# A block scheme with seven products for the MLP's first matmul, and decoding dealt to two passes

## The chip, the cores and the metric

The kernel runs on one core of one Trainium2 chip. The metric is device time in microseconds of one execution; the profile is of one execution. TensorE (PE) multiplies, with its weight loads (PEld) beside it; VectorE (DVE), ScalarE (ACT) and GpSimd (POOL) work on elements; SyncE (SP) issues most DMAs.

## What is computed

Clustered attention over 2 batches, 8 heads, 768 positions of 64, and then two MLP layers over all 1536 tokens (512 wide, 2048 hidden), one behind the other:

```python
x = np.ascontiguousarray(attn_out.transpose(0, 2, 1, 3)).reshape(B * S, H * D)
# layer 1
h = x @ w_in
g = h * (1.0 / (1.0 + np.exp(-1.702 * h)))
x = g @ w_out
# layer 2
h = x @ w_in2
r = np.maximum(h, 0.0)
out = (r * r) @ w_out2
```

The four weight matrices come as 64-bit floats, so the kernel decodes them to 32 bits itself. Every matmul operand is split in two parts of the reduced format `fp32r`, `hi` (a rounded copy) and `lo` (what is left), and every product is three matmuls: hi*hi, hi*lo, lo*hi.

## The kernel before

Attention fills the first third of the span. It also decodes the first weights on the side and leaves x in `x1[b]`, one tile per batch of 768 tokens.

The MLP is four passes: layer 1 for batch 0, layer 1 for batch 1, layer 2 for batch 0, layer 2 for batch 1. A pass goes over 16 chunks of 128 hidden columns. For a chunk, `hidden` (L120) computes the first product into two PSUM banks, 12 matmuls of 512 columns and 12 of 256; `act.gate` (L677) applies the nonlinearity, ScalarE first and then a multiplication on VectorE; `act.split` (L686) makes `gh` on ScalarE and `gl` on VectorE; and `second` (L691) adds the chunk's share of the second product to six PSUM banks. `second` of a chunk is issued after `hidden` of the next one (`pend`), so that gate and split of a chunk have the time of a second product and a first product. At the end of a pass `finish` (L711) copies the six banks to `x1[b]` or stores them to the output. There are 8 banks: two for `hidden`, six for `second`.

A weight chunk is loaded by SP as 64-bit words (`w_dma`, L67, 512 KB, two buffers), ScalarE takes the absolute value (`magnitude`, L76), VectorE makes 32-bit floats of it in four steps (`decode`, L82: clamp, shift, sign, low bits), and `parts` (L100) splits it: ScalarE copies the high half, GpSimd subtracts for the low half. Each chunk of a layer needs this twice, for w_in and for w_out. A layer's decoded chunks stay in SBUF for both batches. The loop at L734 decodes layer 1 in the first pass and layer 2 in the second, one chunk per turn of the loop, in between gate and split in an order written out by hand. Each engine works strictly in the order of issue.

## Time and profile before

| what | value |
|---|---|
| time, median of 3 runs (lowest to highest) | 808.25 us (807.52 to 809.0) |
| the profiled execution: span from first to last instruction | 805.4 us |
| mean granted TensorE clock | 0.999 of full speed |
| mean DMA rate | 76 GB/s |

The page gives the profiled execution by its span; what lies before the first and after the last instruction is not in it. A share of busy time is a mean over stages: attention to about 263 us, then passes from about 270, 401, 536 and 670 us on. In a timeline, "x4" merges four instructions, and a row's duration runs to the end of the last; matmuls are pipelined, so the time that one costs is read from start to next start.

### The profile page before, as it was taken

Reading aid. Unit: us, or ns where it says so; the run is one execution under the profiler, and the core shown is the slowest. Engines: PE = TensorE matmul, PEld = TensorE weight load, DVE = VectorE, ACT = ScalarE, POOL = GpSimd, SP = SyncE. Lnnn points to the kernel's source line nnn. Section 1 sums busy time; section 2 is a strip of 40 time slices with the busy share of each in tenths; the row PEclk is TensorE's granted clock in tenths of the full one; section 3 lists DMA queues with packets and bytes.
Section 4 is the critical chain, followed back from the end, with each engine's and each line's share of the span. In section 5 each row is a group of like instructions: output and inputs, shape, how many; then the busy total and the mean of one; then the engine's idle time right before and its main releaser. Section 6 shows DMA issues by size and latency. Waiting matters only on the chain.

```text
span 805.4 us, 12494 instructions
## 1 busy us (share of the span) xinstructions
PE 794.0 (99%) x4647; PEld 694.2 (86%) x4647; DVE 571.1 (71%) x941; ACT 435.5 (54%) x927; POOL 203.6 (25%) x185
## 2 busy tenths in 40 slices
PE   8999999999999999999999999999999999999998
PEld 5899989989988888888888888888888888888886
DVE  7899999998898699999759999988222234222222
ACT  5898898888989545555534555554222233212222
POOL 1435535445436243323103232312000000000000
PEclk9999999999999999999999999999999999999999
DMA  8242542432311244343204434421000002000002
GB/s 231 87 131 56 161 123 63 136 105 53 82 27 34 74 131 130 117 130 121 79 27 131 128 110 131 130 81 51 1 1 1 0 1 79 1 1 0 1 1 78
DMA packets 40412, 60.89 MB, mean 76 GB/s; under 512 B 4224, under 2 KB 31648, under 8 KB 40352
## 3 DMA queue, kind: packets, MB, share of 16 engines
q1 hardware_dynamic: 35168, 52.98, 22.8%
q10 hardware_dynamic: 5184, 7.12, 2.6%
q8 instruction: 36, 0.59, 0.3%
q14 instruction: 24, 0.20, 0.1%
HBM read 46.18 MB, written 3.19 MB: 61 GB/s over the span
## 4 chain that ended last, share of the span: by engine, by line
PE 82%; DVE 9%; ACT 5%; DMA 2%; issue 1%; POOL 1%; ACTq 0%; DVEq 0%; POOLq 0%; SPq 0%
PE ph L129 31%; PE y L709 16%; PE y L700 10%; PE pa L442 5%; PE pt L417 5%; PE y L702 5%; DVE el L430 3%; PE ps L393 3%; PE ps L394 2%; DVE nm L399 2%; ACT e L408 2%; DMA raw<-in_moe_w_out_dram 1%; PE pt L255 1%; PE ps L279 1%; PE pm L292 1%
## 5 line engine op out<-in xcount | busy, mean ns | idle before, releaser
L684 DVE TENSOR_TENSOR s<-s 128x512 f32<-128x512 f32 x64 | 36.3, 567 | 134.6 <-ACT s L683 134.6
L129 PE MATMUL ph<-xh,ih 128*128 128x512 f32 (+1 forms) x512 | 110.4, 338 | 0.6 <-ACT ih L102 0.4
L129 PE MATMUL ph<-xl,ih 128*128 128x512 f32 (+1 forms) x512 | 110.0, 336 | 0.0
L129 PE MATMUL ph<-xh,il 128*128 128x512 f32 (+1 forms) x512 | 109.6, 336 | 0.0
L688 ACT CAST gh<-s 128x512 fp32r<-128x512 f32 (+1 forms) x128 | 65.6, 513 | 73.9 <-DVE s L684 50.7
L430 DVE TENSOR_TENSOR el<-pt,eh 128x384 fp32r<-128x384 f32 x192 | 97.5, 549 | 8.1 <-ACT eh L427 7.5
L683 ACT ACTIVATE s<-ph 128x512 f32<-128x512 f32 x64 | 31.2, 487 | 129.4 <-PE ph L129 129.4
L689 DVE TENSOR_TENSOR gl<-s,gh 128x512 fp32r<-128x512 f32 (+1 forms) x128 | 71.8, 561 | 40.5 <-ACT gh L688 40.5
L399 DVE TENSOR_REDUCE nm<-ps 128x1 f32<-128x768 f32 x96 | 91.2, 950 | 12.3 <-PE ps L394 11.5
L93 DVE SCALAR_TENSOR_TENSOR dec<-raw,dec 128x512 uint32<-128x512 uint32 x64 | 99.1, 1548 | 1.1
L129 PEld LDWEIGHTS ph<-xh,ih 128*128 128x128 f32 x512 | 84.5, 188 | 15.9 <-ACT ih L102 1.1
L408 ACT ACTIVATE e<-ps,nm 128x768 f32<-128x768 f32 x96 | 88.8, 925 | 13.6 <-DVE rows L474 6.7
L129 PEld LDWEIGHTS ph<-xl,ih 128*128 128x128 f32 x512 | 83.4, 190 | 10.7 <-DVE xl L117 0.4
L129 PEld LDWEIGHTS ph<-xh,il 128*128 128x128 f32 x512 | 83.4, 190 | 10.0
L427 ACT CAST eh<-pt 128x384 fp32r<-128x384 f32 x192 | 84.0, 497 | 9.8 <-PE pt L417 8.8
L417 PE MATMUL pt<-identF,e 128*128 128x128 f32 x576 | 81.7, 276 | 2.4 <-DVE el L430 1.6
L103 POOL TENSOR_TENSOR il<-dec,ih 128x512 fp32r<-128x512 f32 x32 | 41.7, 1303 | 138.7 <-ACT ih L102 121.0
L709 PE MATMUL y<-oh,gh 128*128 128x512 f32 x192 | 75.1, 391 | 0.0
L709 PE MATMUL y<-ol,gh 128*128 128x512 f32 x192 | 75.1, 391 | 0.0
L709 PE MATMUL y<-oh,gl 128*128 128x512 f32 x192 | 74.7, 389 | 0.0
L79 ACT ACTIVATE dec<-raw 128x512 f32<-128x512 f32 x64 | 43.2, 676 | 53.1 <-DMA raw<-in_moe_w_out_dram 28.9
L417 PEld LDWEIGHTS pt<-identF,e 128*128 128x128 f32 x576 | 64.5, 140 | 7.9 <-DVE el L430 7.1
(132 smaller groups left out, 1545.8 us busy)
## 6 DMA issues: line engine op xcount, KB each, us to landing
raw<-in_moe_w_in_dram SPq DMA_DIRECT2D x32, 512.0 KB
raw<-in_moe_w_out_dram SPq DMA_DIRECT2D x32, 512.0 KB, 3.3
k<-k SPq DMA_DIRECT2D x16, 192.0 KB, 2.6
q<-q SPq DMA_DIRECT2D x16, 192.0 KB, 2.5
rr<-row SPq DMA_DIRECT2D x16, 192.0 KB, 3.5
out_dram<-o SPq DMA_DIRECT2D x12, 256.0 KB, 3.0
both<-both SPq DMA_DIRECT2D x30, 96.0 KB, 2.7
rawk<-in_k_dram ACTq DMA_DIRECT2D x6, 384.0 KB, 3.3
```

Of the source, the lines that this page charges most:

```text
L79: nc.scalar.activation(f32(t), f32(raw)[:, :, 1], ACTF.Abs)
L93: nc.vector.scalar_tensor_tensor(out=t, in0=high, scalar=0xC0000000, in1=t, op0=ALU.bitwise_and, op1=ALU.bitwise_or)
L129: nc.tensor.matmul(ph, w[:, kc * P:(kc + 1) * P], xs[kc][z][:, a:a + n], start=(j == 0), stop=(j == len(terms) - 1))
L399: nc.vector.tensor_reduce(out=nm, in_=live["s", t][:, 0:S], op=ALU.max, axis=AX, negate=True)
L408: nc.scalar.activation(e, live["s", t][:, 0:S], ACTF.Exp, bias=live.pop(("nm", t)), accum_out=sums[:, s:s + 1])
L417: nc.tensor.transpose(pt[:, i], e[:, kc * P:(kc + 1) * P], identF)
L427: nc.scalar.copy(place("eh", t, u), live["pt", t, u])
L430: nc.vector.tensor_tensor(out=place("el", t, u), in0=live.pop(("pt", t, u)), in1=f32(place("eh", t, u)), op=ALU.subtract)
L688: nc.scalar.copy(gh, self.s)
L689: nc.vector.tensor_sub(gl, self.s, f32(gh))
L700: nc.tensor.matmul(y[m], l[:, cs], gha if hi else gla, start=first, stop=last)
L709: nc.tensor.matmul(y[m], l[:, cs], r, start=(fc == 0 and z == 0), stop=(fc == KF - 1 and z == 2))
```

## The change

For a pair of chunks the first product is a product of a weight block matrix with an x block matrix: the 512 inputs are halved, the 256 hidden columns of the pair are halved, and the 768 tokens are halved. That makes eight block products of 256 inputs, 128 hidden columns and 384 tokens. The change takes 21 of the 32 pairs with seven products, in the form of Strassen's scheme with common sums: `Combos` holds the x blocks and their four sums (S1 to S4), `Weights` the w_in blocks and their four sums (T1 to T4), each split into hi and lo. Some products add up in a PSUM bank, others are copied to SBUF by ScalarE and added by VectorE.

The first pass (layer 1, batch 0) keeps single chunks. The other three passes are 24 slots of one pair each; the first three slots (`NC`) compute the pair plainly with 384-column matmuls, the other 21 with seven products, A and B being two PSUM banks that change places from slot to slot. The second product of a pair is cut into four parts, issued between the products of the next slot. `finish` is spread over the four parts as well.

The decoded w_in chunks no longer stay in SBUF: `keep` stores each to DRAM (256 KB), and `Weights` loads a pair (512 KB) in the slot ahead. In the first pass `keep` stands ahead of the next load in SP's queue. Layer 2's 32 decodings are tasks dealt to slots 0 to 14 (`COUNTS`). `parts` now subtracts on VectorE; GpSimd has nothing left in the MLP but the last normalisation. The operand sums for a pass are made one per slot in the upper half of the pass before, and their splits mostly in its last slot.

```diff
         nc.scalar.copy(hi, tf)
-        nc.gpsimd.tensor_tensor(out=lo, in0=tf, in1=f32(hi), op=ALU.subtract)
-
-    def w_tiles(fc):
+        nc.vector.tensor_tensor(out=lo, in0=tf, in1=f32(hi), op=ALU.subtract)
...
+    def w_tiles(fc):
+
+        wi = (wx_p if fc % 2 == 0 else wp_b[1]).tile([P, 2, KD * P], F32R, tag="wx", name="wi")
+        return (wi[:, 0, :], wi[:, 1, :]) + out_tiles(fc)
+
+    wst = store.tile([2, KF // 2, P, 2, DM], F32, name="wst")
+
+    def keep(layer, fc, tf):
+
+        nc.sync.dma_start(wst[layer, fc // 2][:, 1 - fc % 2, :], tf)
...
+    xb_p = ctx.enter_context(tc.tile_pool(name="xb", bufs=6))
+    g_p = ctx.enter_context(tc.tile_pool(name="gp", bufs=4))
...
+        units = [(m, i) for m in range(6 if layer else KD) for i in range(len(chunks))]
+        n = len(units) // 4
+        return [lambda k=k: [unit(*u) for u in units[k * n:(k + 1) * n]] for k in range(4)]
...
+        for m in ((0,), (1, 2), (3,), (4, 5))[k]:
+            copies[m % 2](f32(outs[m]), y[m])
+            nc.sync.dma_start(dst[:, m, :], f32(outs[m]))
...
+        A11, A12, S2, S1, S3, S4, A22, A21 = range(8)
...
+        def sum(self, i):
+            dst, x, y, op = ((self.s1, self.a21, self.a22, ALU.add), (self.s3, self.a11, self.a21, ALU.subtract),
+                             (self.s2, self.s1, self.a11, ALU.subtract), (self.s4, self.a12, self.s2, ALU.subtract))[i]
+            nc.vector.tensor_tensor(out=dst, in0=x, in1=y, op=op)
+
+        def part(self, i):
+            src = (self.a11, self.a12, self.s2, self.s1, self.s3, self.s4, self.a22, self.a21)[i]
+            if not self.tiles[i]:
+                self.room(i)
+            hi, lo = self.tiles[i]
+            nc.scalar.copy(hi, src)
+            nc.vector.tensor_tensor(out=lo, in0=src, in1=f32(hi), op=ALU.subtract)
...
+        B11, B21, T1, T2 = range(4)
+        B22, T3, T4 = range(3)
...
+            nc.sync.dma_start(self.wb.rearrange("p (a k) n -> p a (k n)", a=2), wst[layer, p])
+
+        def sums(self):
+            wb, tt = self.wb, nc.vector.tensor_tensor
+            b12, b22, b11, b21 = (wb[:, i, :] for i in range(4))
+            tt(out=wt[:, 0, :], in0=b12, in1=b11, op=ALU.subtract)
+            tt(out=wt[:, 1, :], in0=b22, in1=wt[:, 0, :], op=ALU.subtract)
+            tt(out=wt[:, 2, :], in0=b22, in1=b12, op=ALU.subtract)
+            tt(out=wt[:, 3, :], in0=b21, in1=wt[:, 1, :], op=ALU.subtract)
+
+        def part(self, hi, lo, at, src):
+            nc.scalar.copy(hi[:, at, :], src)
+            nc.vector.tensor_tensor(out=lo[:, at, :], in0=src, in1=f32(hi[:, at, :]), op=ALU.subtract)
+
+        def early(self):
+            hi = wx_p.tile([P, 4, 2 * P], F32R, tag="wx", name="wxh")
+            lo = wp_b[1].tile([P, 4, 2 * P], F32R, tag="wx", name="wxl")
+            self.part(hi, lo, slice(0, 2), self.wb[:, 2:4, :])
+            self.part(hi, lo, slice(2, 4), wt[:, 0:2, :])
+            self.x = hi, lo
+
+        def late(self):
+            hi = wy_p.tile([P, 3, 2 * P], F32R, tag="wyh", name="wyh")
+            lo = wy_p.tile([P, 3, 2 * P], F32R, tag="wyl", name="wyl")
+            self.part(hi, lo, slice(1, 3), wt[:, 2:4, :])
+            self.part(hi, lo, slice(0, 1), self.wb[:, 1:2, :])
+            self.y = hi, lo
...
+    def product(ps, w, wi, x, start=False):
+        terms = [(0, 0), (0, 1), (1, 0)]
+        for j, (a, z) in enumerate(terms):
+            for kc in range(2):
+                nc.tensor.matmul(ps, w[a][:, wi, kc * P:(kc + 1) * P], x[z][:, kc, :],
+                                 start=start and j == kc == 0, stop=j == 2 and kc == 1, skip_group_check=True)
...
+    NC = 3
+    COUNTS = (2, 4, 4, 2, 2, 2, 2, 1, 1, 2, 2, 2, 2, 2, 2, 0)
+    tasks = [(kind, 2 * k + i) for kind, k in (
+        (0, 0), (0, 1), (0, 2), (1, 0), (0, 3), (1, 1), (0, 4), (1, 2), (0, 5), (1, 3), (0, 6), (1, 4), (0, 7),
+        (1, 5), (1, 6), (1, 7)) for i in range(2)]
...
+        tf = decode(*ready[n], steps=(k,) if k < 4 else ())
+        if k == 3:
+            fetch()
+        if k == 4:
+            if kind == 0:
+                keep(1, fc, tf)
+            else:
+                wo2[fc] = out_tiles(fc)
+                parts(tf, *wo2[fc])
...
+            tf = f32(mags[2 * c][1]) if c < 3 else decode(*mag)
+            if c > 1:
+                keep(0, c, tf)
+            if c > 2:
+                if c + 1 < KF:
+                    raw[0] = w_dma(w_in1, c + 1, True)
+                else:
+                    fetch()
...
+                raw[1] = w_dma(w_out1, c + 1, False)
+                mag = magnitude(raw[0]) if c > 1 else None
+            else:
+                fetch()
+            if c > 1:
+                parts(tf, new[2], new[3])
+            if c == 4:
+                last_norm()
+        if fc in (0, 6):
+            combos.part(fc // 6)
...
+        if q < NC:
+            xq = [[x[i] for i in r] for r in ((0, 1), (7, 6))]
+            for c, g in ((0, ga), (1, gb)):
+                for i, at in enumerate((lo_, hi_)):
+                    plain(bank[i], wq.x, c, xq[i])
+                    gate(0, h[:, c, at], bank[i], s[:, at])
+                    if 2 * c + i < n:
+                        absolute()
+                    nc.scalar.copy(g[0][:, at], h[:, c, at])
+                    do(2 * c + i, (0, 1))
+                    nc.vector.tensor_sub(g[1][:, at], h[:, c, at], f32(g[0][:, at]))
+                    do(2 * c + i, (2, 3, 4))
+                    if i:
+                        for k in (2 * c, 2 * c + 1):
+                            pend[k]()
+                            ending(k)
+                        if q < NC - 1:
+                            wn.plain(c, wq.x)
+                            combos.sum(2 * q + c)
+                        elif not c:
+                            wn.sums()
+                            combos.part(4)
+                        else:
+                            wn.early()
+                            combos.part(2)
...
+        product(A, wq.x, wq.B11, x[Combos.A11], True)
+        wq.late()
+        if q == NC:
+            combos.part(3)
+        nc.scalar.copy(p1, A)
+        if n:
+            absolute()
+        if p == NP - 1 and q + 1 < len(slots):
+            nxt.room(3, 4, 5, 6)
+            nxt.part(0)
+        product(B_, wq.x, wq.B21, x[Combos.A12], True)
+        nc.vector.tensor_tensor(out=h[:, 0, lo_], in0=B_, in1=p1, op=ALU.add)
+        do(0, (0, 1))
+        gated(layer, h[:, 0, lo_], s[:, lo_])
+        do(0, (2, 3))
+        split(ga, h[:, 0, :], lo_)
+        pend[0]()
+        ending(0)
+        product(A, wq.x, wq.T2, x[Combos.S2])
+        nc.scalar.copy(u2, A)
+        product(B_, wq.x, wq.T1, x[Combos.S1], True)
+        nc.scalar.copy(p5, B_)
+        do(0, (4,))
+        if p == 0 or q == NC:
+            combos.part(5)
+        if p == NP - 1 and q + 1 < len(slots):
+            nxt.part(1)
+        if n > 1:
+            absolute()
+        if q + 1 < len(slots):
+            wn.sums()
+            wn.early()
+        if p == 0:
+            combos.part(6)
+        pend[1]()
+        ending(1)
+        do(1, (0, 1))
+        if p == NP - 1 and q + 1 < len(slots):
+            nxt.part(2)
+        product(A, wq.y, wq.T3, x[Combos.S3])
+        nc.vector.tensor_tensor(out=h[:, 1, hi_], in0=A, in1=p5, op=ALU.add)
+        product(B_, wq.y, wq.B22, x[Combos.S4])
+        nc.vector.tensor_tensor(out=h[:, 1, lo_], in0=B_, in1=u2, op=ALU.add)
+        do(1, (2, 3))
+        gated(layer, h[:, 1, :], s)
+        do(1, (4,))
+        split(gb, h[:, 1, :])
+        pend[2]()
+        ending(2)
+        product(A, wq.y, wq.T4, x[Combos.A22])
+        gate(layer, h[:, 0, hi_], A, s[:, hi_])
+        split(ga, h[:, 0, :], hi_)
+        if q < 2 * NP and p > 3:
+            if p == 4:
+                nxt = Combos(slots[q + NP][1])
+            nxt.sum(p - 4)
+        if p == NP - 1 and q + 1 < len(slots):
+            nxt.part(3)
+            nxt.part(4)
+        pend[3]()
+        ending(3)
...
+    for k in range(4):
+        pend[k]()
+        finish(*ends, k)
```

## Rows read from the trace of the kernel before

**Rows 1.** The profile's page, part 1: busy time and share of the span, instructions of each engine.
```profile
PE 794.0 (99%) x4647; PEld 694.2 (86%) x4647; DVE 571.1 (71%) x941; ACT 435.5 (54%) x927; POOL 203.6 (25%) x185
```

**Rows 2.** Busy time by stretch: start and end, length; engines, granted clock, DMA share, GB/s.
```profile
401.00:535.70 134.70, 134.66 (x768) 117.67 (x767) 119.57 (x180) 67.86 (x126) 36.22 (x28) 1.00 0.36 110
...
668.00:803.00 135.00, 133.57 (x679) 113.91 (x677) 37.93 (x70) 33.46 (x69) 0.00 (x0) 1.00 0.06 21
```

**Rows 3.** Timeline of TensorE, one chunk of layer 1, one of layer 2: start, duration, instruction.
```profile
422.76 1.09 PE L129 MATMUL ph<-xh,ih 128*128 128x512 f32 x4
...
426.94 0.40 PE L700 MATMUL y<-gh,oh 128*128 128x512 f32 x1
...
431.18 1.09 PE L129 MATMUL ph<-xh,ih 128*128 128x512 f32 x4
...
566.05 1.07 PE L129 MATMUL ph<-xh,ih 128*128 128x512 f32 x4
...
570.20 0.40 PE L709 MATMUL y<-oh,gh 128*128 128x512 f32 x1
...
574.31 1.07 PE L129 MATMUL ph<-xh,ih 128*128 128x512 f32 x4
```

**Rows 4.** Six 384-column matmuls of attention and what follows; their weight loads by group.
```profile
161.81 1.21 PE L442 MATMUL pa<-el,v 128*128 128x384 f32 x6
162.86 0.38 PE L255 MATMUL pt<-identR,nat 128*128 128x128 f32 x3
...
L442 PEld LDWEIGHTS pa<-el,v 128*128 128x128 f32 x192 | 32.9, 189 | 0.0
```

**Rows 5.** Timeline of VectorE, and one row of GpSimd, whose start lies beside the fifth.
```profile
279.54 0.69 DVE L93 SCALAR_TENSOR_TENSOR dec<-raw,dec 128x512 uint32<-128x512 uint32 x1
280.27 0.69 DVE L96 SCALAR_TENSOR_TENSOR dec<-raw,dec 128x512 uint32<-128x512 uint32 x1
280.88 0.42 DVE L88 TENSOR_SCALAR dec<-dec 128x512 f32<-128x512 f32 x1
281.33 0.43 DVE L90 TENSOR_SCALAR dec<-dec 128x512 uint32<-128x512 uint32 x1
281.79 1.75 DVE L93 SCALAR_TENSOR_TENSOR dec<-raw,dec 128x512 uint32<-128x512 uint32 x1
...
281.70 1.30 POOL L103 TENSOR_TENSOR ol<-dec,oh 128x512 fp32r<-128x512 f32 x1 [4.34 <-ACT oh L102]
...
427.77 0.68 DVE L689 TENSOR_TENSOR gl<-s,gh 128x512 fp32r<-128x512 f32 x1
428.38 0.42 DVE L681 TENSOR_TENSOR s<-ph,s 128x256 f32<-128x256 f32 x1
428.71 1.73 DVE L93 SCALAR_TENSOR_TENSOR dec<-raw,dec 128x512 uint32<-128x512 uint32 x1
...
264.30 1.02 DVE L430 TENSOR_TENSOR el<-pt,eh 128x384 fp32r<-128x384 f32 x2 [0.18 <-ACT eh L427]
...
395.97 3.56 DVE L117 TENSOR_TENSOR xl<-x,xh 128x768 fp32r<-128x768 f32 x4 [0.31 <-ACT xh L116]
```

**Rows 6.** Timeline of VectorE: a subtraction behind ScalarE's copy; in brackets the idle time before it.
```profile
410.94 0.69 DVE L689 TENSOR_TENSOR gl<-s,gh 128x512 fp32r<-128x512 f32 x1 [0.69 <-ACT gh L688]
```

**Rows 7.** A w_in load's issue, the absolute value behind it, and a stretch of the DMA engines.
```profile
292.55 0.38 SPq L70 DMA_DIRECT2D raw<-in_moe_w_in_dram  x1
...
296.38 0.68 ACT L79 ACTIVATE dec<-raw 128x512 f32<-128x512 f32 x1 [0.71 <-DMA raw<-in_moe_w_in_dram]
...
433.00:434.00 1.00, 1.00 (x6) 0.82 (x5) 1.00 (x1) 0.00 (x0) 0.47 (x1) 1.00 0.95 352
```

**Rows 8.** First pass: TensorE's start of a chunk, and VectorE's first gating of that chunk.
```profile
304.46 1.20 PE L129 MATMUL ph<-xh,ih 128*128 128x512 f32 x4 [0.40 <-ACT ih L102]
...
310.49 0.68 DVE L681 TENSOR_TENSOR s<-ph,s 128x512 f32<-128x512 f32 x1
```

More of the change, by code (lines that the diff above doesn't have):

```diff
@@ L691, in second, with g_tiles, split, gate @@
-    def second(layer, y, g, w, fc):
-        (gha, gla), (ghb, glb) = g
-        oh, ol = w[2], w[3]
-        if layer == 0:
-            for m in range(KD):
+    def g_tiles():
+        return g_p.tile([P, S], F32R, tag="gh", name="gh"), g_p.tile([P, S], F32R, tag="gl", name="gl")
+    def split(g, src, at=slice(0, S)):
+        gh, gl = g
+        nc.scalar.copy(gh[:, at], src[:, at])
+        nc.vector.tensor_sub(gl[:, at], src[:, at], f32(gh[:, at]))
+    def gate(layer, dst, src, tmp):
+        if layer == 0:
+            nc.scalar.activation(tmp, src, ACTF.Sigmoid, scale=1.702)
+            nc.vector.tensor_mul(dst, src, tmp)
+        else:
+            nc.scalar.activation(tmp, src, ACTF.Relu)
+            nc.vector.tensor_mul(dst, tmp, tmp)
@@ L696, in second, with gated, unit @@
+    def gated(layer, dst, tmp):
+        if layer == 0:
+            gate(layer, dst, dst, tmp)
+        else:
+            nc.vector.scalar_tensor_tensor(out=dst, in0=dst, scalar=0.0, in1=dst, op0=ALU.max, op1=ALU.mult)
+    def second(layer, y, chunks):
+        def unit(m, i):
+            (gh, gl), (oh, ol), fc = chunks[i]
+            if layer == 0:
                 cs = slice(m * P, (m + 1) * P)
                 yb = y[4 + m // 2][:, m % 2 * 256:m % 2 * 256 + 256]
-                for z, (l, hi) in enumerate(((oh, 1), (ol, 1), (oh, 0))):
+                for z, (l, r) in enumerate(((oh, gl), (ol, gh), (oh, gh))):
@@ L708, in second @@
                 for z, (l, r) in enumerate(((gh, oh), (gh, ol), (gl, oh))):
[L709 to L720 removed]
+                    nc.tensor.matmul(y[m], l[:, m * P:(m + 1) * P], r,
+                                     start=(fc == 0 and z == 0), stop=(fc == KF - 1 and z == 2))
@@ new lines, in tile_kernel, with act @@
+    wo1 = {0: w1[2:]}
+    w = w1
+    y = y_tiles()
+    pend = None
+    combos = Combos(1, True)
+    weights = {}
+    for fc in range(KF):
+        c = fc + 1
+        new = w_tiles(c) if c < KF else None
+        if new:
+            wo1[c] = new[2:]
+            tf = f32(mags[2 * c][1]) if c < 3 else decode(*mag)
[4 more added lines that the diff above has]
+                    raw[0] = w_dma(w_in1, c + 1, True)
+                else:
+                    fetch()
+        g = g_tiles()
+        cut = (slice(0, 512), slice(512, S))
+        def act(i):
+            gate(0, s[:, cut[i]], first[i] if fc == 0 else hidden(xs, w, i), s[:, cut[i]])
+        act(0)
+        if new and c == 1:
+            parts(tf, new[0], new[1])
+        if new and c > 2:
+            mag = magnitude(raw[1])
+            decode(*mag, steps=(0, 1))
+        split(g, s, cut[0])
+        act(1)
+        if new and c > 1:
+            parts(tf, new[0], new[1])
+            if c > 2:
+                decode(*mag, steps=(2,))
+        split(g, s, cut[1])
+        if new:
+            if c == 2:
+                mag = magnitude(raw[1])
+                decode(*mag, steps=range(3))
+            tf = decode(*mag, steps=(3,)) if c > 1 else f32(mags[3][0])[:, :, 0]
+            if c == 1:
+                parts(tf, new[2], new[3])
+            if c + 1 < KF:
+                raw[1] = w_dma(w_out1, c + 1, False)
+                mag = magnitude(raw[0]) if c > 1 else None
+            else:
+                fetch()
+            if c > 1:
+                parts(tf, new[2], new[3])
+            if c == 4:
+                last_norm()
+        if fc in (0, 6):
+            combos.part(fc // 6)
+        if fc == 12:
+            weights[0, 0] = Weights(0, 0)
+            tmp12 = rpool.tile([P, S], F32, tag="rr", name="p12")
+        if pend:
+            for part in pend:
+                part()
+        pend = second(0, y, [(g, wo1[fc], fc)])
+        w = new
```

206 lines of the change are left out of this document (107 added, 99 removed).

## The prediction

> **What bounds the kernel now.** I read the busy times first: TensorE is busy 794.0 of 805.4 us, VectorE 71% and ScalarE 54% [rows 1]. Shares are means over stages, so the stretches came next. In the second MLP pass (401 to 535.7 us) TensorE has no gap and VectorE is busy 119.6 of 134.7 us; in the last pass VectorE is busy 37.9 of 135 us and TensorE still has no gap before the tail [rows 2]. So the MLP costs what its matmuls cost, while VectorE is nearly full wherever weights are decoded. In the timeline of TensorE a layer-1 chunk is 4.18 us of first product and 4.24 us of second, a layer-2 chunk 4.15 and 4.11 us [rows 3]. Fewer matmul columns are worth their full time only where VectorE can keep step.
>
> All sums are made against the span, 805.4 us. The median of the runs is 808.25 us, 2.85 us more, which I take as lying around the span and unchanged.
>
> **What the scheme saves.** A first product for two chunks is now 48 matmuls, 24 of 512 and 24 of 256 columns. A pair in the block scheme has seven products of six 384-column matmuls, 42. Six such matmuls in attention stand 1.05 us from first to next, 0.175 us each, each with its own weight load [rows 4]; by columns (4.15 us for 12 times 768) it would be 0.173. I take 0.174: a product is 1.04 us, seven are 7.31 us. Against 8.36 us in layer 1 that saves 1.05 us in 5 slots, against 8.30 us in layer 2 0.99 us in 16: **21.1 us**. The three plain slots (48 of 384 columns, 8.35 us) change nothing, nor does the new order inside the second product: the same matmuls, so a slot has 8.48 us of them in layer 1 and 8.22 in layer 2. A block-scheme slot is therefore 15.8 or 15.5 us of TensorE.
>
> The Trainium skill ("TensorE: Matmul & The Clock Gate", Back-to-back issue gap) gives N/2.4 + 2.5 ns for an isolated warm matmul, an estimate of 162.5 ns at 384 columns; by it a pair would save 0.98 us and 21 pairs 20.5. The rows are slower than it, 175 ns, and are used. The same page (Part 3, What overlaps and what doesn't) says that a weight load overlaps running matmuls only in another row group, which would speak against more matmuls per column; here full-array loads of 190 ns run beside matmuls spaced 175 ns apart, so this trace disagrees.
>
> **VectorE's prices.** Start to next start: 256 columns 0.33 us, 512 columns 0.61, 768 columns 0.86 (four in 3.56 us), 384 columns 0.47 (two in 1.02). The four decoding steps cost 0.45 + 0.46 + 0.73 + 0.61 = 2.25 us with GpSimd idle; with a GpSimd subtraction beside it the third takes 1.75 us instead of 0.69 [rows 5]. Moving the subtraction of `parts` to VectorE thus adds 0.61 us and takes off up to 1.06 us: cheap in work. What it costs is order: VectorE now waits for ScalarE's copy before it, as it sat 0.69 us for the copy of a 512-column gate [rows 6].
>
> **First pass (16 chunks, unchanged matmuls).** VectorE now does the low half of w_out in its own queue, and ahead of it ScalarE has the next w_in's absolute value, which waits for that load. The loop, from the end of a w_in decoding: SP issues `keep` first (0.4), then the load, which today lands 3.8 us after its issue [rows 7]; the 256 KB of `keep` go ahead of it on the same engines, and I add 0.3. That is 4.5; absolute value 0.67, wait for the copy 0.6, subtraction 0.6, next decoding 2.3: 8.7 us against 8.42 of TensorE. Bounds: 8.43 if the store costs no more than its issue, 9.1 if its bytes delay the load in full (256 KB at 352 GB/s [rows 7] are 0.7 us). Nothing hides it: VectorE's first gating of a chunk today starts 6.0 us after the chunk, the next chunk's weights are copied after it, and TensorE waited 0.40 us for such a copy at 304.46 [rows 8]. So 12 loops at 0.3 = 3.6 us, plus 0.86 for an operand split in chunk 6, less 0.4 of slack at the start and 0.4 for the wait that goes: **3.7 us lost**, bounds 0 and 9.
>
> **The slots.** Layer 2's 32 decodings, today in the second pass, are dealt as 2, 4, 4, 2, 2, 2, 2, 1, 1 and six times 2 to slots 0 to 14, so half of them meet the scheme's own work. VectorE in a block-scheme slot: seven 384-column operations (3.3), two of 768 (1.7), three of 512 (1.8), five of 256 (1.65), together 8.5 us; ScalarE's answers before two of the subtractions 1.6 (1.0 where a w_out subtraction fills one); two decodings 4.5; two w_out subtractions 1.2 where the pair is w_out; one operand sum 0.86 in the upper half of a pass. So 14.6 to 15.5 us for w_in pairs, 15.2 to 16.1 for w_out pairs, beside 15.5 to 15.8 of TensorE. I went through the slots in issue order. TensorE tolerates about 2.5 us of lag: a bank is wanted again after a quarter of the second product and one block product (3.1 us), less the sum that frees it.
> - Slot 2 to 3: from 2.8 us into slot 2 VectorE has eight gatings and subtractions (3.8), four decodings (9.0), two w_out splits with ScalarE's answer (2.6), four weight sums (1.3), an operand split (0.9) and the next weights' low halves; the first of these ends near 21.1 us, while TensorE needs it at 17.5: **3.6 us**.
> - Slot 3 starts 2.3 us late, with two more operand splits: 1.0 at the sum before the last product, 0.9 before the second product of slot 4: **1.9 us**.
> - Slot 5 (w_out pair, operand sum): **0.7 us**.
> - Slots 7 and 8, the change of pass: five operand splits (4.3 us) beside one decoding, then two splits, one decoding and the copies out of the finished sums: 2.0 and 3.6 us, **5.6 us**.
> - Slots 13 to 15: three w_out pairs with sums, then five splits: **2.0 us**.
> From slot 16 on VectorE has under 12 us of 15.5: nothing. Together **13.8 us**. Bounds: 6, if half of ScalarE's answers are hidden and operations overlap; 20, if each of 13 slots is half a us longer.
>
> **At no cost.** DMAs: 32 stores of 256 KB and 24 loads of 512 KB are more than the old traffic, but the reloads are issued a slot ahead, after the previous slot's fetches in SP's queue, some 6 us before VectorE adds them up; without that cover a slot would wait some 4 us. ScalarE stays under 11 us a slot; its copies sit behind TensorE's products, not ahead of them. Copies out of finished sums are spread over a slot; their banks are wanted a slot later. The tail keeps its last copy and store. Unseen in any row is a matmul that adds to a bank after the bank was read: between nothing and the 0.40 us of rows 8 once in each of 21 slots, 8 us; I take nothing, as in rows 3 the first matmul into a bank that others have read starts without a gap.
>
> **The sum:** 21.1 - 3.7 - 13.8 = 3.6 us gained; span 801.8, time 804.6 us.
>
> **Rivals.**
> 1. VectorE keeps step: 793 us. If ScalarE's answers hide and the first pass holds 8.42 us, only the hand-over (3.6) and half of the change of pass (2.8) remain: 21.1 - 6.4 + 0.4 = 15.1. For: sums of 14.6 to 16.1 beside 15.5 to 15.8 leave it open. Against: the waits in rows 6 and 9. Chance 0.30.
> 2. VectorE sets the pace of slots 3 to 14: 814 us, slower. Sums that free the banks are queued behind decoding steps, which wait for absolute values, which wait for loads. 0.8 us more in each of 12 slots is 9.6. It decides from 0.45 us a slot on, a mean slot of 16.9 us where mine is 16.4. For: VectorE in the second pass is 89% busy today with less to do. Against: the third decoding step gets 1 us shorter. Chance 0.17.
> 3. The 384-column products don't run at 0.174 us: if the weight load set the pace (0.19), 882 matmuls would cost 14 us more, 818 us. Rows 4 speak against. Chance 0.03.
>
> **Numbers.** The forecast (798 to 810 us) has 0.50. The range: rivals 1 and 2 from their near side, 790 to 814. A measurement of this kernel can tell about 0.2%, 1.6 us. Faster by more: 0.36 of the forecast, rival 1 and 0.02 of rival 2's edge: 0.68. Within: 0.10. Slower: 0.04 of the forecast, rival 2's rest and rival 3, rounded to 0.22.
>
> **What would show it.** In the new profile: six 384-column matmuls in 1.04 to 1.05 us; no GpSimd work once the last normalisation is done and the third decoding step near 0.69 us; chunks of the first pass 8.7 us apart with TensorE waiting for the `ih` copy; slots of 15.5 us from slot 17 on; TensorE waiting on VectorE at the starts of slots 3 and 8, and hardly elsewhere. A first pass at 8.42 us and mean slots 3 to 15 under 16 us make rival 1; over 16.9 rival 2.

## The result and the profile after

Four runs of the changed kernel have a median of 813.2 us (811.91 to 815.76), four of the kernel before on the same chip 807.88 (807.06 to 809.0): a ratio of 1.0073, with a 95% interval of 1.0053 to 1.0092. The kernel became slower by 5.3 us, where 3.6 us of gain were predicted. The profiled execution took 813.53 us; its span is 811.7 us, 6.3 more than before.

The first line of the page's part 1 (busy time of each engine), and of its part 4 (the chain of work that ended last, by engine):

```profile
PE 784.2 (97%) x4521; PEld 697.9 (86%) x4521; DVE 666.0 (82%) x1202; ACT 478.2 (59%) x1004; POOL 121.9 (15%) x121
...
PE 52%; DVE 27%; ACT 10%; DMA 5%; issue 4%; POOL 1%; ACTq 0%; SPq 0%; DVEq 0%; POOLq 0%
```

Against [rows 1] TensorE is busy 9.8 us less and VectorE 94.9 us more. TensorE's work did not grow, its waiting did: 27.5 us of the span it now stands idle, where it stood 11.4 before. The longest of its waits tell for whom it stands (engine and line, who is waited for: us in total, times, longest). `h` at L1045 is VectorE's sum that frees a bank for a slot's last product, `wi` ScalarE's copy of the next chunk's weights in the first pass, `wxh` its copy of the scheme's first weights, `el` a piece of attention:

```profile
PE ps L832 <- DVE h L1045: 5.1, 5, 1.7
PE ph L140 <- ACT wi L104: 3.1, 4, 1.7
PE ps L832 <- ACT wxh L805: 2.9, 1, 2.9
PE pt L428 <- DVE el L441: 2.8, 9, 0.4
```

VectorE holds 27% of the chain that ended last. The slots show where. The starts of the 24 slots are read from TensorE's timeline, a wait at a start counted to the slot that it opens (columns as in [rows 2]). Slots 3 to 8, 13, 15, 16 and 17 are:

```profile
450.87:473.91 23.04, 19.19 (x92) 17.09 (x91) 20.47 (x38) 12.27 (x22) 0.00 (x0) 0.85 0.40 116
473.91:490.44 16.53, 15.97 (x92) 14.53 (x91) 14.45 (x27) 8.60 (x17) 0.00 (x0) 1.00 0.46 143
490.44:506.05 15.61, 15.61 (x93) 14.62 (x92) 13.69 (x27) 8.81 (x17) 0.00 (x0) 1.00 0.26 87
506.05:522.39 16.34, 16.00 (x92) 14.53 (x91) 14.64 (x28) 8.39 (x17) 0.00 (x0) 1.00 0.43 134
522.39:539.70 17.31, 15.88 (x93) 14.58 (x91) 14.36 (x26) 9.76 (x18) 0.00 (x0) 1.00 0.32 114
539.70:559.53 19.83, 16.91 (x92) 14.41 (x91) 17.61 (x30) 11.21 (x21) 0.00 (x0) 1.00 0.16 54
...
622.33:638.45 16.12, 15.99 (x80) 14.07 (x78) 15.03 (x28) 7.56 (x16) 0.00 (x0) 1.00 0.27 89
...
654.73:671.70 16.97, 16.26 (x79) 14.01 (x78) 13.56 (x23) 8.24 (x16) 0.00 (x0) 1.00 0.10 31
671.70:689.39 17.69, 16.19 (x79) 13.98 (x78) 14.09 (x25) 9.27 (x17) 0.00 (x0) 1.00 0.12 45
689.39:705.10 15.71, 15.71 (x79) 14.13 (x78) 11.12 (x21) 6.97 (x14) 0.00 (x0) 1.00 0.35 118
```

A scheme slot in which TensorE never waits is 15.60 us in layer 1 (slot 5; in the row its ends are rounded) and 15.71 in layer 2 (slots 10 to 12, and 17 on; slot 9 is 15.68). Two chunks before were 16.84 and 16.52 us [rows 3]. So a scheme slot saves 1.24 us in each of 5 pairs and 0.81 in each of 16: **19.2 us**. The three plain slots are 16.64 us undisturbed, 0.6 in all less than six chunks before. Above these undisturbed lengths the slots lose 0.5 in slots 0 and 1, 7.4 in slot 3 (wait included), 0.9 in slot 4, 0.7 in slot 6, 1.7 in slot 7, 4.2 in slot 8, 0.4, 0.6 and 1.3 in slots 13 to 15, and 2.0 in slot 16: **19.7 us**. That alone uses up the saving.

The 19.2 us hold a change of the second product too. The last product of slots 5 and 10, and a quarter of the second product behind it:

```profile
502.93 0.85 PE L832 MATMUL ps<-x,wyh 128*128 128x384 f32 x4
503.97 0.39 PE L721 MATMUL y<-gl,oh 128*128 128x512 f32 x1
506.05 0.85 PE L832 MATMUL ps<-x,wxh 128*128 128x384 f32 x4
...
587.77 0.87 PE L832 MATMUL ps<-x,wyh 128*128 128x384 f32 x4
588.84 0.39 PE L727 MATMUL y<-oh,gh 128*128 128x512 f32 x1
590.92 0.87 PE L832 MATMUL ps<-x,wxh 128*128 128x384 f32 x4
```

Six 384-column matmuls take 1.04 us in layer 1 and 1.05 to 1.07 in layer 2. A second product, four such quarters of 2.08 us, takes 8.32 us in both layers. Before, two chunks had 8.48 us in layer 1 and 8.22 in layer 2 [rows 3], so the same matmuls, now in another order and cut into parts, became 0.16 us a pair shorter in layer 1 and 0.1 longer in layer 2.

Slot 3 is the dearest. TensorE's timeline from the last matmul of slot 2 on, and then stretches of 1 us of the same time:

```profile
450.75 0.28 PE L723 MATMUL y<-gh,oh 128*128 128x256 f32 x1
453.88 1.65 PE L832 MATMUL ps<-x,wxh 128*128 128x384 f32 x4 [2.85 <-ACT wxh L805]
456.01 1.01 PE L832 MATMUL ps<-x,wxl 128*128 128x384 f32 x2 [0.48 <-DVE wxl L806]
456.82 1.48 PE L832 MATMUL ps<-x,wxh 128*128 128x384 f32 x4
...
461.67 0.87 PE L832 MATMUL ps<-x,wxh 128*128 128x384 f32 x4
462.38 0.51 PE L832 MATMUL ps<-x,wxl 128*128 128x384 f32 x2
462.73 0.85 PE L832 MATMUL ps<-x,wxh 128*128 128x384 f32 x4
```

```profile
452.00:453.00 1.00, 0.00 (x0) 0.00 (x0) 1.00 (x3) 0.20 (x1) 0.00 (x0) 1.00 0.00 0
453.00:454.00 1.00, 0.12 (x1) 0.12 (x1) 0.97 (x4) 1.00 (x3) 0.00 (x0) 0.87 0.77 102
454.00:455.00 1.00, 1.00 (x3) 1.00 (x4) 0.97 (x3) 1.00 (x3) 0.00 (x0) 0.50 0.85 221
...
460.00:461.00 1.00, 1.00 (x7) 0.86 (x6) 0.97 (x4) 0.27 (x2) 0.00 (x0) 0.71 0.46 184
461.00:462.00 1.00, 1.00 (x8) 0.91 (x7) 0.96 (x2) 0.51 (x1) 0.00 (x0) 1.00 0.03 8
```

TensorE stands 2.85 us for the scheme's first weights, VectorE being busy all that time. Then it works at a granted clock of 0.50 (1.2 of 2.4 GHz) until 460.6 us: six matmuls stand some 1.9 us apart in place of 1.06 (461.67 to 462.73).

In the first pass the chunks, which before stood 8.42 us apart as in [rows 3], begin at 8.42 and then mostly stand 8.6 to 8.9 us apart, and two far more: 10.24 us at 306.13, behind a late load, and 9.69 at 325.21, after the operand split of chunk 6 that the prediction had priced at 0.86. TensorE's chunk starts:

```profile
306.13 1.09 PE L140 MATMUL ph<-xh,wi 128*128 128x512 f32 x4
316.37 1.21 PE L140 MATMUL ph<-xh,wi 128*128 128x512 f32 x4 [1.66 <-ACT wi L104]
...
378.76 1.20 PE L140 MATMUL ph<-xh,wi 128*128 128x512 f32 x4
387.44 1.21 PE L140 MATMUL ph<-xh,wi 128*128 128x512 f32 x4
```

From the chunk at 280.87 us to slot 0 at 404.64 are 14 intervals, 123.8 us; 14 times 8.42 are 117.9. That is 5.9 us lost, against 0.7 in the kernel before: **5.2 us**.

Attention, which no term of the prediction held, ends later: the first hidden product starts at 265.60 us and not at 263.29, **2.3 us**. VectorE's timeline shows the two subtractions of `parts` that now stand in its queue there:

```profile
65.28 0.82 DVE L105 TENSOR_TENSOR wi<-dec,wi 128x512 fp32r<-128x512 f32 x1 [0.81 <-ACT wi L104]
...
98.01 0.81 DVE L105 TENSOR_TENSOR ol<-dec,oh 128x512 fp32r<-128x512 f32 x1 [0.81 <-ACT oh L104]
```

The balance: 19.2 + 0.6 saved, and 1.1 that the kernel before lost at its changes of pass; 2.3 + 5.2 + 19.7 lost. That makes 6.3 us more, as the span has it.

### The profile page after: what moved, and what is told of

It is laid out like the page before. It is cut to its first block, busy times and chain, and to the rows that moved or that the text cites. A ratio compares the mean times of both kernels' runs of the same rounds, so it can differ in the third digit from the quotient of the medians.

```text
span 811.7 us, 12557 instructions
## 1 busy us (share of the span) xinstructions
PE 784.2 (97%) x4521; PEld 697.9 (86%) x4521; DVE 666.0 (82%) x1202; ACT 478.2 (59%) x1004; POOL 121.9 (15%) x121
## 4 chain that ended last, share of the span: by engine, by line
PE 52%; DVE 27%; ACT 10%; DMA 5%; issue 4%; POOL 1%; ACTq 0%; SPq 0%; DVEq 0%; POOLq 0%
PE ps L832 12%; PE y L727 12%; PE pa L453 5%; PE pt L428 5%; DMA raw<-in_moe_w_in_dram 4%; PE ph L140 4%; PE y L721 3%; PE ps L404 3%; DVE el L441 3%; DVE dec L98 2%; DVE nm L410 2%; PE ps L405 2%; DVE dec L95 2%; DVE wxl L806 2%; PE y L723 2%
## 5 line engine op out<-in xcount | busy, mean ns | idle before, releaser
L419 ACT ACTIVATE e<-ps,nm 128x768 f32<-128x768 f32 x96 | 88.7, 924 | 16.9 <-DVE nm L410 9.6
L832 PE MATMUL ps<-x,wxh 128*128 128x384 f32 x336 | 74.4, 343 | 5.5 <-ACT wxh L805 2.9
L404 PE MATMUL ps<-k,q 80*128 80x512 f32 x192 | 70.3, 366 | 0.5 <-ACT k L371 0.5
L696 DVE TENSOR_TENSOR gl<-h,gh 128x384 fp32r<-128x384 f32 (+1 forms) x63 | 43.5, 691 | 32.7 <-ACT gh L695 32.7
L81 ACT ACTIVATE dec<-raw 128x512 f32<-128x512 f32 x64 | 43.1, 673 | 45.0 <-DMA raw<-in_moe_w_out_dram 15.9
L832 PEld LDWEIGHTS ps<-x,wxh 128*128 128x128 f32 x336 | 59.9, 191 | 11.0 <-ACT wxh L805 3.2
L405 PE MATMUL ps<-k,q 128*128 128x512 f32 x192 | 61.2, 340 | 0.0
L832 PE MATMUL ps<-x,wyh 128*128 128x384 f32 x252 | 55.3, 340 | 5.7 <-DVE h L1045 5.1
L140 PE MATMUL ph<-xh,wi 128*128 128x512 f32 (+1 forms) x256 | 53.7, 342 | 3.3 <-ACT wi L104 3.1
L832 PEld LDWEIGHTS ps<-x,wyh 128*128 128x128 f32 x252 | 44.0, 188 | 11.5 <-DVE h L1045 4.4
L721 PE MATMUL y<-gh,ol 128*128 128x512 f32 x128 | 51.0, 399 | 0.0
L721 PE MATMUL y<-gl,oh 128*128 128x512 f32 x128 | 50.8, 397 | 0.0
```

What stands on the lines that cost most here:

```text
L140: nc.tensor.matmul(ph, w[:, kc * P:(kc + 1) * P], xs[kc][z][:, a:a + n], start=(j == 0), stop=(j == len(terms) - 1))
L404: nc.tensor.matmul(ps[:, a:a + n], q1[0:K1, qs], k1[0:K1, a:a + n], start=True, stop=False)
L405: nc.tensor.matmul(ps[:, a:a + n], q2[:, qs], k2[:, a:a + n], start=False, stop=True)
L419: nc.scalar.activation(e, live["s", t][:, 0:S], ACTF.Exp, bias=live.pop(("nm", t)), accum_out=sums[:, s:s + 1])
L696: nc.vector.tensor_sub(gl[:, at], src[:, at], f32(gh[:, at]))
L721: nc.tensor.matmul(y[m], l[:, cs], r[:, 0:512], start=first, stop=last)
```

## The experiments

Each kernel is the changed one with the edit shown, unless it says otherwise. Each was timed in five rounds beside the kernel before; a time is the median, and the interval is of the ratio to the kernel before.

**Attention's two subtractions back on GpSimd (a1).**

```diff
-                        parts(f32(mags[i][1]), w1[2 * m], w1[2 * m + 1])
+                        parts(f32(mags[i][1]), w1[2 * m], w1[2 * m + 1], nc.gpsimd)
```

> Edit: only the two parts calls inside the attention loop go back to GpSimd; all later ones stay on VectorE. Theory (VectorE stands in its queue for ScalarE's copy in attention and delays the pieces el that TensorE needs): the attention ends about 2.3 us earlier, the first hidden product starts at about 263.3 instead of 265.6 us, and the kernel takes about 810.9 us. Rival (the attention is later for another reason, or the wait only changes place): 813.2 us, hidden product still at 265.6.

Measured: 810.62 us (1.0022 to 1.0051), 2.6 us less than the changed kernel. The first hidden product starts at 264.12 us, 1.5 earlier, less than the 2.3 expected. Over the changed kernel and its versions below it started at 264.95 to 267.43 us in ten profiles with these subtractions on VectorE (mean 265.83), and at 263.52 to 264.81 in four with them on GpSimd (mean 264.17). The theory holds; by these profiles the cost is nearer 1.7 us than 2.3.

**The load ahead of the store in SP's queue (a2).**

```diff
-            if c > 1:
-                keep(0, c, tf)
             if c > 2:
                 ...
+            if c > 1:
+                keep(0, c, tf)
```

> Edit: in the first pass the load of the next w_in chunk is issued ahead of the store of the decoded chunk in SyncE's queue. Theory (the loop decode, store issue, load issue, landing, Abs, copy, subtract sets the pace of the first pass): each of ten chunk intervals falls from about 8.7 to 8.4 us, the pass to the first slot shortens by about 3 us, kernel 810.2 us. Rival (landing alone or ScalarE sets the pace, or the store that is now later holds up the tile it is read from): intervals stay at 8.7 us, kernel 813.2 us.

Measured: 819.16 us (1.0118 to 1.0145), 6 us more. The intervals grew to 9.3 us. ScalarE's timeline shows why:

```profile
386.94 0.67 ACT L81 ACTIVATE dec<-raw 128x512 f32<-128x512 f32 x1 [2.37 <-DMA wst<-dec]
```

The decoded chunk lies in one of two `dec` tiles. The absolute value of the next chunk writes that tile, and so waits for the store to have read it. With the store first, its 2.5 us (median, from issue to landing) lie under the load's 4; behind the load it takes 4.5. The theory falls: the rival that named the held tile is right, though it expected the intervals to stay at 8.7.

**Two tasks from slot 2 to slot 0 (a3).**

```diff
-    COUNTS = (2, 4, 4, 2, 2, 2, 2, 1, 1, 2, 2, 2, 2, 2, 2, 0)
+    COUNTS = (4, 4, 2, 2, 2, 2, 2, 1, 1, 2, 2, 2, 2, 2, 2, 0)
```

> Edit: two decoding tasks of slot 2 move to slot 0 (four tasks in slots 0 and 1, two in slot 2). Theory (four tasks of decoding in slot 2 make the scheme's first weights late and TensorE waits 2.9 and 0.5 us for them, after which it runs at a granted clock of 0.50): the waits at the start of slot 3 and the fall of the clock both go, slot 3 falls from 23.0 to about 16.5 us, slot 0 grows by at most 0.5, kernel about 807 us. Rival (the scheme's own sums and splits, not the decoding, make the weights late): the wait stays over 2 us, the kernel at 812 or more.

Measured: 812.7 us (1.0041 to 1.0076). Half of the theory held: slot 3 starts without a wait and takes 16.41 us, so decoding is what made the first weights late. But the lag only moved. TensorE now waits at the starts of slots 1 and 2:

```profile
421.87 1.68 PE L839 MATMUL ps<-x,wxh 128*128 128x384 f32 x8 [2.57 <-DVE h L701]
...
440.62 2.54 PE L839 MATMUL ps<-x,wxh 128*128 128x384 f32 x8 [1.82 <-DVE h L701]
```

The kernel gained nothing clear of noise. Eight decodings in a row, six of them of w_in with its store, don't fit in two slots: ScalarE's absolute values waited 1.3 to 3.0 us, five times, for stores out of the `dec` tiles, and VectorE behind them. After the second of these stops the granted clock was 0.50 here too:

```profile
442.00:444.00 2.00, 2.00 (x8) 2.00 (x8) 1.23 (x3) 0.76 (x2) 0.00 (x0) 0.50 0.00 0
```

**TensorE kept at work through the wait (a4).**

```diff
+        if q == NC:
+            for _ in range(13):
+                nc.tensor.matmul(y[0], zr, gprev[0][:, 0:512], start=False, stop=False, skip_group_check=True)
         product(A, wq.x, wq.B11, x[Combos.A11], True)
```

> Edit: thirteen products of zeros are put between the last product of slot 2 and the first of slot 3, where TensorE waits 2.9 us for the scheme's first weights; they add zero to a bank and need no late data. Theory (about 3 us of slot 3's 23.0 are the lower granted clock of 453.9 to 460.6 us, which follows the idle stretch): with TensorE kept at work the clock stays at 1.00, slot 3 takes about 20 us, kernel about 810.2 us. Rival (the low clock lies in time in which VectorE would have made TensorE wait anyway): the clock stays up but the products wait, slot 3 stays near 23 us, kernel 813.2 us.

Measured: 810.93 us (1.0024 to 1.0048), 2.3 us less. The 13 products fill the wait, and the granted clock stays at 1.00:

```profile
450.35 3.15 PE L1012 MATMUL y<-gh,zr 128*128 128x512 f32 x13
453.33 0.95 PE L832 MATMUL ps<-x,wxh 128*128 128x384 f32 x4
455.44 0.62 PE L832 MATMUL ps<-x,wxl 128*128 128x384 f32 x2 [1.16 <-DVE wxl L806]
```

```profile
453.30:460.00 6.70, 5.54 (x31) 4.96 (x31) 6.63 (x13) 4.37 (x8) 0.00 (x0) 1.00 0.92 295
```

Slot 3 from its first product on falls from 20.03 to 18.00 us, not by 3: one wait, for the low halves, grew from 0.48 to 1.16. So the theory holds, and the low clock cost 2.0 us net of that wait.

**First pass's subtractions back on GpSimd (b1), and all of them (b2).** The edit is that of a1, at the calls in the first pass, and in `parts` itself.

> Edit: the parts calls of the first pass alone go back to GpSimd; attention and the slots keep them on VectorE. Theory (the subtraction of the w_out parts, which stands on VectorE ahead of the next decoding, waits 1.3 us for ScalarE's copy and takes 0.7; these two lie in the loop decode, store, load, landing, Abs that sets the pace): chunk intervals fall from 8.7 to 8.4 us, the first pass by 3 to 4 us, kernel about 809.5 us. Rival (the loads' landing, or steps that GpSimd slows while it shares its port with VectorE, keep the pace): intervals stay at 8.7 us or more, kernel 813 us or more.

Measured: 813.09 us (1.0050 to 1.0079), nothing gained.

> Edit: every parts call is on GpSimd again, in attention, in the first pass and in the 16 decoding tasks of the slots: that part of the change is undone. Theory (it cost more than it freed): attention gives back 2.3 us, the first pass 3.5, and in the slots 16 subtractions of 0.69 us leave VectorE, where they were late only in the slots that wait, so 1 to 3 us more; kernel about 806 us. Rival (in the slots GpSimd's subtraction slows VectorE's own steps, since the row of before has a step of 0.69 us at 1.75 beside it): slots are slower by some 5 us, kernel 811 us or more.

Measured: 812.71 us (1.0048 to 1.0078). Attention came out 1.4 us shorter, the first pass 1.3 longer (0.8 longer in b1), and in the slots the gains (0.4 each in slots 6 and 13) are outweighed by losses (0.5 each in slots 7 and 8, 0.2 and 0.3 in slots 3 and 14): 0.8 longer in all. Both theories fall. In b1 the steady intervals do shrink, from 8.68 to 8.50 us, but a decoding step beside GpSimd takes 1.51 us in place of 0.69 again, as in [rows 5], and early in the pass TensorE waited 1.2 to 1.6 us three times:

```profile
388.30 1.51 DVE L95 SCALAR_TENSOR_TENSOR dec<-raw,dec 128x512 uint32<-128x512 uint32 x1
```

**The decoding steps left out of the slots (b3).**

```diff
-        tf = decode(*ready[n], steps=(k,) if k < 4 else ())
+        tf = f32(ready[n][1])
```

> Edit: in the slots the four decoding steps of each of the 32 chunks are left out (some 72 us of VectorE); loads, absolute values, parts and stores stay, so the second layer's weights are not the decoded ones. Theory (VectorE's queue, the scheme's own sums and splits with the decoding between them, makes products late in slots 3, 4, 6, 7, 8 and 13 to 16): with the decoding gone the waits of slots 3 and 6 to 8 go, together about 12 of the 16 us lost in slots 3 to 16, kernel about 801 us; what is left stands at the changes of pass, slots 8 and 16, where the scheme's own operands are made. Rival (the dependence of the scheme's products on one another, copies on ScalarE or the stores and loads set these waits): the slots keep their times within 3 us in all, kernel 810 us or more.

Measured: 799.92 us (0.9889 to 0.9915), 13.3 us less. Slots 3, 7, 8 and 16:

```profile
449.09:464.69 15.60, 15.60 (x92) 14.62 (x91) 10.70 (x19) 9.25 (x17) 0.00 (x0) 1.00 0.47 160
...
512.22:528.72 16.50, 15.90 (x92) 14.64 (x91) 11.97 (x21) 9.63 (x18) 0.00 (x0) 1.00 0.19 64
528.72:547.89 19.17, 16.72 (x92) 14.47 (x91) 15.76 (x26) 11.20 (x21) 0.00 (x0) 1.00 0.16 56
...
658.12:675.81 17.69, 16.21 (x80) 13.99 (x78) 14.10 (x25) 9.26 (x17) 0.00 (x0) 1.00 0.12 45
```

The theory holds, a little more strongly than expected. The hand-over (slots 2 to 3) is free without decoding, and slots 6, 13 and 14 run at TensorE's pace. What stays is mostly the change of pass: 3.5 us in slot 8 and 2.0 in slot 16, where VectorE has the scheme's own operand splits and the copies out of finished sums and no decoding; 0.7 and 0.9 us also stay in slots 4 and 7.

**The scheme one slot later (b4).** `NC` is 4, and the sums of batch 1 are still made in the first two slots.

> Edit: the scheme begins one slot later (four plain chunk pairs instead of three, 20 pairs by the scheme instead of 21); the tasks of each slot stay, so the last plain slot decodes two chunks instead of four. Theory (the hand-over is late because of the decoding beside it): one pair by the scheme less costs 1.2 us, the wait of 3 us at the hand-over and the low clock behind it go, 5 to 6 us, kernel about 808.5 us. Rival (the hand-over is late by the scheme's own first weights and operands): the wait only moves by one slot and the kernel takes 814.4 us.

Measured: 810.44 us (1.0022 to 1.0047), 2.8 us less, although one pair is plain again (16.64 us for 15.60). The result lies between theory and rival: the hand-over moved by one slot and shrank but did not go. The first scheme slot waits 1.86 us, and the granted clock behind this shorter stop stayed at 1.00.

**The scheme in layer 2 alone (c1).** The eight slots of layer 1 are plain pairs and take 22 of the 32 decodings; the sums for layer 2's first operands are made in slots 4 to 7.

```diff
-    NC = 3
-    COUNTS = (2, 4, 4, 2, 2, 2, 2, 1, 1, 2, 2, 2, 2, 2, 2, 0)
+    NC = 8
+    COUNTS = (2, 4, 3, 4, 3, 4, 2, 0, 0, 2, 2, 2, 2, 2, 0, 0)
...
                         if q < NC - 1:
                             wn.plain(c, wq.x)
-                            combos.sum(2 * q + c)
                         elif not c:
                             wn.sums()
-                            combos.part(4)
+                            nxt.room(3, 4, 5, 6)
+                            for i in (0, 3, 4):
+                                nxt.part(i)
                         else:
                             wn.early()
-                            combos.part(2)
+                            nxt.part(1)
+                            nxt.part(2)
...
```

> Edit: the scheme in layer 2 alone (16 pairs); the eight slots of layer 1 are plain pairs and take most of the decoding (2, 4, 3, 4, 3, 4, 2, 0 chunks, then five times 2 in slots 9 to 13); operands of the first scheme slot are made in slot 7. Theory (a plain slot leaves VectorE room for decoding, a scheme slot doesn't): slots 1 to 7 take 16.7 us each, 117 in place of 122.2, although five pairs lose the 1.2 us of the scheme; slot 8 falls by about 2 us, slots 13 to 15 by 1.5; kernel about 805 us. Rival (the wait at the beginning of the scheme and at changes of pass is the scheme's own, and a slot cannot decode 3 or 4 chunks in a row, because each store must end before the buffer is written again): slots 2 to 6 take over 17.5 us and slot 8 over 20, kernel 812 us or more.

Measured: 802.45 us (0.9919 to 0.9948): 10.8 us less than the changed kernel and 5.5 less than the kernel before. Slots 2, 4 and 8:

```profile
431.81:448.45 16.64, 16.64 (x98) 15.66 (x97) 13.38 (x26) 7.21 (x15) 0.00 (x0) 1.00 0.56 177
465.09:482.23 17.14, 16.80 (x98) 15.54 (x97) 14.47 (x27) 7.58 (x16) 0.00 (x0) 1.00 0.56 180
...
532.28:548.96 16.68, 15.93 (x93) 14.59 (x91) 12.61 (x22) 8.33 (x16) 0.00 (x0) 1.00 0.09 31
```

The theory holds, by more than expected. Plain pairs in place of five by the scheme cost 5.2 us (16.64 for 15.60 each). Even so slots 1 to 7, from first product to first product, take 117.1 us in place of 122.2, and slot 8 16.7 in place of 19.8: plain slots with three or four chunks of decoding wait 0.6 us in all.

**The same, with attention's subtractions on GpSimd and the copies out of finished sums on ScalarE (c3).**

```diff
-            finish(*ends, k, copies=(nc.scalar.copy, nc.vector.tensor_copy if q else nc.scalar.copy))
+            finish(*ends, k, copies=(nc.scalar.copy, nc.scalar.copy))
```

> Edit: the scheme in layer 2 alone as in the run beside it, the attention's two subtractions on GpSimd again, and the copies out of finished sums on ScalarE alone. Theory: 2.3 us less than the run beside it from attention, and 0.5 to 1 us each at slots 8 and 16, where VectorE's two or three copies stand ahead of the sum that TensorE waits for; about 801.5 us. Rival (ScalarE's copies come later than VectorE's would and hold the banks of the second product): attention's 2.3 us alone, or slots 8 and 16 longer, 803 us or more.

Measured: **798.71 us** (0.9876 to 0.9905), the fastest version, 1.1% under the kernel before. The theory holds: slot 8 falls to 16.04 and slot 16 to 17.11 us, 0.6 each, and the first hidden product starts at 263.52.

**The stores from GpSimd's queue (d1).**

```diff
-        nc.sync.dma_start(wst[layer, fc // 2][:, 1 - fc % 2, :], tf)
+        nc.gpsimd.dma_start(wst[layer, fc // 2][:, 1 - fc % 2, :], tf)
```

> Edit: the stores of decoded w_in chunks are issued from GpSimd's queue instead of SyncE's. Theory (the store's issue and bytes ahead of the load in one queue are what makes the first pass's loop 8.7 us): the load is issued 0.4 us earlier, intervals fall to 8.4 to 8.5 us, the first pass by 2 to 3 us, kernel about 811 us. Rival (the load and the store share the DMA engines, so the load lands later or the store ends later and the next absolute value waits for it, as it did with the load issued first): intervals of 8.7 us or more, kernel 813 us or more.

Measured: 817.38 us (1.0098 to 1.0128). The rival is right, and it is a2's wait again: a store now takes 4.6 us to land and not 2.5, and the absolute value waits for it:

```profile
367.46 0.66 ACT L81 ACTIVATE dec<-raw 128x512 f32<-128x512 f32 x1 [2.26 <-DMA wst<-dec]
```

**The first pass without its stores (e1).** Chunks 2 to 15 of layer 1 are not stored, and all layer-1 slots load the first pair.

```diff
-            if c > 1:
-                keep(0, c, tf)
...
-            nc.sync.dma_start(self.wb.rearrange("p (a k) n -> p a (k n)", a=2), wst[layer, p])
+            nc.sync.dma_start(self.wb.rearrange("p (a k) n -> p a (k n)", a=2), wst[layer, p if layer else 0])
```

> Edit: the first pass stores no w_in chunks (chunks 2 to 15 of layer 1 are left out of the DRAM copy, and the slots of layer 1 all load the first pair in their place, so batch 1 of layer 1 is computed with wrong weights). Theory (the store's issue and bytes are the term that takes the loop over TensorE's 8.42 us): intervals fall to 8.42 to 8.45 us, the first pass by 4 to 5 us, kernel about 809 us. Rival (VectorE's order, with the subtraction waiting for ScalarE between two decodings, is enough by itself): intervals stay above 8.6 us, kernel 812 us or more.

Measured: 808.21 us (0.9996 to 1.0016), 5.0 less than the changed kernel. Every interval of the pass is 8.42 us:

```profile
340.21 1.09 PE L140 MATMUL ph<-xh,wi 128*128 128x512 f32 x4
...
348.63 1.09 PE L140 MATMUL ph<-xh,wi 128*128 128x512 f32 x4
```

So without the store the first pass loses nothing, the operand split of chunk 6 included. The subtractions on VectorE lie in the same loop (b1's steady intervals fell to 8.50 us without them), but by themselves they cost TensorE nothing here. The load is now issued 0.07 us after the decoding ends, where it stood 0.42 us behind the store's issue, and the absolute value starts 3.70 to 3.77 us after it, where it started 4.04 to 4.15. How much of the loss is the issue and how much the landing, no run separates.

**The kernel before with `parts` on VectorE, nothing else (e2).**

> Edit: the kernel before, with the subtraction of parts on VectorE instead of GpSimd and nothing else: that part of the change alone. Theory (its cost in order is attention's 2.3 us; in the first pass, with no store in the loop, TensorE hides it): kernel 810 us, the first hidden product 2 us later, chunk intervals 8.42 us. Rival (the subtractions on VectorE cost the first two passes too): over 812 us with intervals above 8.42. Rival (the third decoding step gets so much shorter that VectorE is ahead everywhere): 808 us.

Measured: 808.25 us (1.0002 to 1.0019), 0.4 us more than before. Its first hidden product starts 2.2 us late, at

```profile
265.53 1.17 PE L129 MATMUL ph<-xh,ih 128*128 128x512 f32 x4
```

but the chunks of its first pass stand 8.42 us apart without exception; it gets back the 0.7 us that the kernel before lost in that pass (one wait of it in [rows 8]) and some 0.5 at the next change of layer. The time is that of the second rival, 808 us, although attention is late as the theory said: later stages give most of it back. By itself the move costs next to nothing in the kernel's time.

**The fastest version with the first pass's subtractions on GpSimd (e3).**

> Edit: the version with the scheme in layer 2 alone, attention's subtractions on GpSimd and copies on ScalarE, with the first pass's subtractions on GpSimd too; the slots keep theirs on VectorE. Theory (by the steady intervals of the earlier run, 8.50 for 8.68 us): the first pass shortens by 1 to 2 us, kernel about 797.5 us. Rival (GpSimd's slowing of VectorE beside the last normalisation and the first splits gives it back, as it did there): 798.7 us or more.

Measured: 801.14 us (0.9895 to 0.9925), 2.4 us more than c3. The gain of 1 to 2 us is not there: two early intervals are over 10 us (10.05 and 10.07), as in b1. A loss of 2.4 is not shown either. The five times fall in two groups, 798.5 to 798.6 and 801.1 to 801.9 us, and c3's four in the same two, three at 798.3 to 798.8 and one at 801.28; that one is its profile's, where the first pass took 125.2 us, and it took 124.4 here. What parts the groups stays open.

## Why the prediction was wrong

The mechanism was right: the scheme saves TensorE's time, and VectorE gives it back in the first pass and in certain slots. But the terms for the costs were too small, the saving was a little too large, and attention's cost was put at nothing, so the sign came out wrong. Against the predicted span of 801.8 us the measured one is 9.9 higher:

- **"21.1 us" saved** was 19.2. In layer 2 a scheme slot is 15.71 us, not 15.5; in layer 1 it is 15.60, not 15.8. Six 384-column matmuls took the predicted 1.04 us in layer 1 and 1.05 to 1.07 in layer 2. The Trainium skill ("TensorE: Matmul & The Clock Gate", Back-to-back issue gap) gives 0.98 by its formula for isolated matmuls, an estimate; the trace is slower. What failed besides is that the new order inside the second product changes nothing: a pair's second product became 0.16 us shorter in layer 1 and 0.1 longer in layer 2. In all that is 1.9 us; whether the order or the cutting into parts did it is not shown.
- **"At no cost"** for attention failed. The prediction priced `parts` in the MLP alone, though the same function is called in attention's loop; that is 2.3 us by the trace, 2.6 by the time of the run that undid it, and 1.7 by the mean of all profiles. The row that should have warned is one of its own [rows 6]: VectorE waits for ScalarE's copy in order.
- **First pass, 3.7 predicted, 5.2 measured.** The loop was right to 0.1 us (8.7), and so was its reason, as the run without stores shows. What was missing is that a loop without slack passes on each late load: one w_in load took 5.9 us to land, and TensorE waited 1.66 us. In c1's profile, where that load was not late, the pass lost 3.9 us in place of 5.9.
- **The slots, 13.8 predicted, 19.7 measured.** Slots 7 and 8 (5.6 predicted, 5.9 measured) and 13 to 15 (2.0 and 2.3) were right. The hand-over with slots 3 and 4 was put at 3.6 + 1.9 and took 8.3. The wait itself was nearly right, 2.85 + 0.48 us for 3.6; 2.0 us of the rest are the granted clock of 0.50 behind it, which the prediction did not think of. **"From slot 16 on ... nothing"** failed by 2.0 us: the prediction summed VectorE's work over the slot, but the operand splits and the copies out of sums come bunched ahead of the sum that frees a bank; with those copies on ScalarE (c3) the slot lost 0.6 less. Half a us stood in slots 0 and 1, where it had nothing. "Slot 5: 0.7" came in slot 6.
- In its favour the prediction left out the 0.6 us of the plain slots and the 1.1 us that the kernel before lost.

Rival 2, VectorE sets the pace of slots 3 to 14, gave 814 us, close to the 813.2 measured, but not by its mechanism. The mean of those slots, from 450.87 to 654.73 us, is 17.0, above the 16.9 from which it decides. But the prediction's own 16.4 comes out of its terms only without the 3.6 us of the hand-over; counted so, from slot 3's first product at 453.88, the mean is 16.7 and rival 2 is not met. Five of the twelve slots lose nothing, and 7.4 of the 15.9 us lost there are slot 3: it is not a pace, it is places where work bunches. Rival 1 would have needed most of the losses that b3 removes to be absent. Rival 3 was not seen: 0.174 to 0.178 us a matmul, not 0.19. (The "rows 9" that the prediction sets against rival 1 are no group of rows.)

One thing stays open: why a w_in load of the first pass took 5.9 us to land. A chunk interval near 10 us at that place stands in several profiles and not in all, and in none without the stores.

## What to carry over

When work moves to an engine that is "only" 70 to 80% busy, a sum over a slot is too coarse: list its queue up to each instruction that frees something another engine needs, and look for places where the work bunches, such as the start of a scheme and a change of pass. A helper function's cost is to be counted at every call, in the stages that the change was not about as well. A block scheme that trades multiplications for additions pays where the adding engine has room: here the same scheme in 16 pairs instead of 21, with the decoding put into the plain pairs, turned a loss of 0.7% into a gain of 0.7%, and of 1.1% with two small moves more.
